# Key blocks of 56 + 8 keys, two heads on the partition halves, in an attention and mixture-of-experts kernel

## The chip, the cores and the metric

The kernel runs on one core of one Trainium2 chip. The metric is the device time of one execution in microseconds (us), lower is better. The core has a matrix engine (TensorE; PE in the profile, with its weight loads listed as PEld), a vector engine (VectorE, DVE), an activation engine (ScalarE, ACT), a general engine (GpSimd, POOL) and a queue (SP) from which this kernel starts nearly all of its DMA transfers. The engines run side by side; each takes its own instructions in program order.

## What is computed

Windowed attention with a few global keys, then a soft mixture of experts over the result:

```python
B, H, S, D = 4, 8, 768, 64          # batch, heads, positions, head size
scores = q @ k.T / sqrt(D)          # per batch and head, 768 x 768
rel  = pos[:, None] - pos[None, :]
keep = (pos[None, :] < 8) | ((rel >= 0) & (rel < 96))      # n_global = 8, n_local = 96
dist = where(is_global & ~is_local, 96, abs(rel))
a = softmax(where(keep, scores - slope[h] * dist, -1e9))
x = (a @ v) -> (B * S, 512)
logits = x @ phi                    # 8 experts x 4 slots = 32 columns
d = softmax(logits, over tokens);  c = softmax(logits, over slots)
slot_out[e] = relu((d.T @ x)[e] @ w1[e]) @ w2[e]           # 512 -> 1024 -> 512
out = c @ slot_out
```

A query sees its 96 most recent keys and the first 8, so of a 768 x 768 score matrix only a band and eight columns are needed.

## The kernel before

**Tiling of the attention.** The work is cut into 16 units `u`, one for each batch and pair of heads. For a unit, the keys are cut into NJ = 7 blocks of KB = 120 (the last has 48). A block of 120 keys is seen by the QW = 120 + 96 = 216 queries from its first key on. The 8 global keys ride along with every block, so a block has KR = 128 rows: 128 partitions of the score tile, with 216 queries along the free axis. A head has 5 x 216 + 168 + 48 = 1296 columns of this kind, a pair 2592.

**The steps of a unit**, each a function that `ORDER` calls by name:

- `load_qk`, `load_v`: SP starts the loads of queries and keys (two buffers, `raw0`, `raw1`) and of values (one buffer, `vraw`, line 420).
- `scores` (lines 530 to 539), in 3 pieces a unit: float32 matmuls on PE, contraction over the 64 rows of one head (the two heads lie on partitions 0 to 63 and 64 to 127), 128 keys out, written to PSUM with the head as bank. Each such matmul has two records in the trace.
- `biased` (line 548), 3 pieces: DVE adds the bias and mask table to the scores, writes SBUF (`tb0` to `tb2`) and keeps a running maximum; `max_t`, `max_r`, `max_b`, `max_c` turn that into one subtrahend for the unit.
- `exponential` (568, ACT), one a head. `w_hi` (578, ACT) rounds the weights to float16; `w_lo` (586, POOL, a few on DVE), 3 pieces a head, takes the float16 rest, so that three float16 products stand for a float32 one.
- `v_hi` (519 on POOL or 522 on ACT) and `v_lo` (527, DVE) split the values in the same way. Both read `vraw`, and the next `load_v` writes it.
- `values` (lines 591 to 603), one a head: for each of 7 tiles of 120 queries, the block of the same keys and the one before, times 3 products: 13 x 3 = 39 float16 matmuls with 128 rows of contraction and 65 or 64 columns.
- `ev_sum`, `ev_rec`, `ev_mul` (609, 613, 619, DVE): row sums, reciprocal, normalised output, for each head; `tr`, `tr_copy` (631, 636): transposes; `logits` (661) and, once a batch, the softmax over tokens and `dispatch` (736).

**Queues and order.** The order of all of this is written out by hand in the list `ORDER`; each engine and SP follow it. The list also places the loads of the expert weights: `piece` k (1 MB each) into one of NW = 12 tiles that are free from the start, and `free` i, which loads weight columns into a buffer of the attention as soon as its last user is done. `load_v` carries one small leftover piece.

**Buffers.** PSUM has 8 banks of 512 float32 columns. The score tiles take 4 (two tiles of two banks), the outputs of `values` one for each head, the rest two. There is one buffer `hi0` and one `lo0` for the split weights (NHB = 1), three for the biased scores (NTB = 3).

**After the attention**: `last_dispatch`, then `hidden` (line 119) with w1, `project` (149) with w2, `combine` (209 to 215), and the output.

```python
for i in range(2):                       # before, in scores: the heads of one block
    r = slice(D * i, D * i + D)
    nc.tensor.matmul(out=sc[:, i, at:at + n], lhsT=r_[r, KCOL[j]:KCOL[j] + KR],
                     rhs=r_[r, KW + KB * j:KW + KB * j + n], start=True, stop=True)
```

Of the kernel before, what the change touches and what calls it, by code (L numbers as in the profile page):

```python
# [23 lines left out]
NG = 8  # L24
KB = 120
P = 128
NJ = 7
KR = NG + KB
WIN = 96
QW = KB + WIN  # L30
QN = (QW,) * 5 + (S - 5 * KB, S - 6 * KB)
TN = tuple(min(KB, S - KB * j) for j in range(NJ))
BANK_J = ((0, 1), (2, 3), (4, 5, 6))
COL = tuple(sum(QN[:j]) for j in range(NJ))
BW = 2 * QW
TW = 3 * BW
TBW = 2 * TW
PB = KB + P
PCOL = tuple(PB * j for j in range(6)) + (PB * 5 + QN[5],)
PW = PCOL[6] + P  # L40
KW = NJ * KR
KCOL = tuple(KR * ((j + 5) % NJ) for j in range(NJ))
Q1 = KB + QW
# [4 lines left out]
XH = NJ * HF  # L48
VHW = NJ * 2 * (D + 1) // 2
VC = NJ * 2 * D  # L50
TABW = 4 * QW
NW = 12
NTB = 3
NHB = 1
# [6 lines left out]
P_EXP = 15  # L61
RS_MIN = 2.0 ** (P_EXP + 6 - 10)
RS_EPS = 1.0e-9 * RS_MIN
X_MIN = 2.0 ** -9


def homes(QKW, TBW, HPW, VC, VW, TABW, XH):
    return [
        ("wa", 12, dict(tab1=TABW, tab2=TABW, raw0=QKW, raw1=QKW, tab0=TABW, tab3=TABW, vraw=VC, tb1=TBW, tb2=TBW, tb0=TBW, v0=VW, v1=VW, hi0=HPW, lo0=HPW, xt1=S, xt2=S, xt0=S, xn2=XH)),
    ]  # L70


leaves = ('tab1', 'tab2', 'raw0', 'raw1', 'tab0', 'tab3', 'vraw', 'tb1', 'tb2', 'tb0', 'v0', 'v1', 'hi0', 'lo0', 'xt1', 'xt2', 'xt0', 'xn2')


T_SC = 0.125
TAB_UNIT = 0.5 / T_SC


class Moe:  # L80


    def __init__(self, tc, ident, sgn):
        self.nc, self.ident, self.sgn = tc.nc, ident, sgn

# [111 lines left out]
    def combine(self, ps, ct, n, sot, obs, out, t0, sizes):  # L197
# [4 lines left out]
        for size in sizes:  # L202
            obs.append(obs.pop(0))
            ob = obs[-1][:, 0:w * size]
            for m in range(0, size, 2):
# [5 lines left out]
                if (t0 + m) // 2 % 2 == 0:  # L211
                    nc.scalar.copy(out=dst, in_=cp)  # L212
                else:
                    nc.vector.tensor_copy(out=dst, in_=cp)  # L214
            nc.sync.dma_start(
                out=out[P * t0:P * (t0 + size), at:at + w].rearrange("(t p) f -> p t f", p=P), in_=ob.rearrange("p (t f) -> p t f", f=w))
            t0 += size


class BiasTable:  # L220

    def __init__(self, nc, tabs, space):

        self.nc, self.tabs = nc, tabs
        at = [0]

        def temp(rows, cols, dtype=F32):
            v = space[0:rows, at[0]:at[0] + cols]  # L230
            at[0] += cols
            return v if dtype == F32 else v.bitcast(dtype)

        def iota(rows, base, pattern, mult):
            i = temp(rows, pattern[1], I32)
            nc.gpsimd.iota(i, pattern=[pattern], base=base, channel_multiplier=mult)
            f = temp(rows, pattern[1])
            nc.vector.tensor_copy(out=f, in_=i)
            return f

        self.rel = iota(P, NG, [1, QW], -1)
        self.grel = iota(NG, 0, [1, QW], -1)
        self.gidx = iota(NG, 0, [0, 1], 1)
        self.other = temp(NG, QW)
        nc.gpsimd.memset(self.other, NEG)
        nc.gpsimd.memset(self.other[:, 0:KB], 0.0)
        self.base = temp(P, QW)
        self.t = temp(P, QW)
        self.g = temp(NG, QW)
        self.l = temp(NG, QW)  # L250
        self.s = temp(NG, 2)
        self.later = temp(P, QW // 2, BF16)
        nc.vector.tensor_scalar(out=self.t, in0=self.rel, scalar1=0.0, scalar2=NEG, op0=ALU.is_lt, op1=ALU.mult)
        nc.vector.scalar_tensor_tensor(out=self.base, in0=self.rel, scalar=-TAB_UNIT, in1=self.t, op0=ALU.mult, op1=ALU.add)

    def keys(self, ngl, nlo):
        nc = self.nc
        nc.vector.tensor_scalar(out=self.t, in0=self.rel, scalar1=nlo, scalar2=NEG, op0=ALU.is_ge, op1=ALU.mult)
        nc.vector.tensor_scalar(out=self.l, in0=self.grel, scalar1=nlo[0:NG], scalar2=NEG, op0=ALU.is_lt, op1=ALU.mult)
        nc.vector.tensor_scalar(out=self.s[:, 0:1], in0=self.gidx, scalar1=ngl[0:NG], scalar2=NEG, op0=ALU.is_ge, op1=ALU.mult)  # L260
        nc.vector.tensor_tensor(out=self.later, in0=self.base, in1=self.t, op=ALU.add)
        nc.vector.scalar_tensor_tensor(out=self.l, in0=self.grel, scalar=0.0, in1=self.l, op0=ALU.is_ge, op1=ALU.mult)
        nc.vector.scalar_tensor_tensor(out=self.s[:, 1:2], in0=nlo[0:NG], scalar=-TAB_UNIT, in1=self.s[:, 0:1], op0=ALU.mult, op1=ALU.add)

    def even(self):
        nc = self.nc
        t0, later = self.tabs[0][:, 0], self.later
        nc.vector.tensor_scalar(out=self.g, in0=self.other, scalar1=self.s[:, 1:2], scalar2=None, op0=ALU.add)
        nc.vector.tensor_copy(out=t0[:, 0:QW], in_=later)
        nc.vector.tensor_copy(out=later[0:NG], in_=self.g)  # L270
        nc.vector.tensor_tensor(out=t0[0:NG, 0:QW], in0=self.g, in1=self.l, op=ALU.add)
        nc.vector.tensor_copy(out=t0[:, QW:3 * QW].rearrange("p (j c) -> p j c", c=QW), in_=later.unsqueeze(1).to_broadcast([P, 2, QW]))
        for at, n in ((0, QN[5]), (QN[5], QN[6])):
            nc.vector.tensor_copy(out=t0[:, 3 * QW + at:3 * QW + at + n], in_=later[:, 0:n])

    def part(self, p, k):

        t = self.tabs[p]
        return bass.AP(tensor=t.tensor, offset=t.offset + QW * k, ap=[t.ap[0], [4 * QW, 2], [1, BW]])

    def odd(self):
        t = self.tabs[0]
        self.nc.vector.tensor_scalar(out=t[:, 1], in0=t[:, 0], scalar1=0.5, scalar2=None, op0=ALU.mult)

    def pair(self, p, act):
        if act:
            self.nc.scalar.activation(out=self.tabs[p], in_=self.tabs[0], func=AF.Copy, scale=0.25 ** p)
        else:
            self.nc.gpsimd.tensor_scalar(out=self.tabs[p], in0=self.tabs[0], scalar1=0.25 ** p, scalar2=0.0, op0=ALU.mult, op1=ALU.add)


@with_exitstack
def tile_attention_moe(ctx: ExitStack, tc: tile.TileContext, qk, v, phi, w1, w2, nn, out):
# [31 lines left out]
    QKW, HPW = S + KW, PW  # L325
# [27 lines left out]
    tabs = [own(f"tab{p}", TABW).bitcast(BF16).rearrange("p (i c) -> p i c", i=2) for p in range(NP)]  # L353
    by_head = "p (j i d) -> p j i d"
    vraw = own("vraw", VC).rearrange(by_head, j=NJ, i=2)
    v16 = [own(f"v{i}", VW) for i in range(2)]
    vhi = [w[:, 0:VHW].bitcast(F16).rearrange(by_head, j=NJ, i=2) for w in v16]
    vlo = [w[:, VHW:].bitcast(F16).rearrange(by_head, j=NJ, i=2) for w in v16]
    xn2 = own("xn2", XH)
    xnb = [a[0:KB].rearrange("p (t f) -> p t f", t=NJ) for a in (xn01[:, 0:XH], xn01[:, XH:], xn2)]  # L360
    xtb = [own(f"xt{i}", S) for i in range(3)]


    last = nu - 1
    spaces = []
# [40 lines left out]
    def free(i):  # L406
        for k, c0, c1 in spaces[i]:
            load_w([NW + held.index(k)], c0, c1)

    FIRST = slice(KCOL[0], KW + Q1)  # L410

    def load_qk0(u):
        nc.sync.dma_start(out=rq[0][:, FIRST], in_=qk[0, 0][:, FIRST])

# [28 lines left out]
    def blocks_of(w, i):  # L443
        return w[:, PW * i:PW * i + 6 * PB].rearrange("p (s c) -> p s c", c=PB)

# [696 lines left out]
```

## Time and profile before

| | us |
|---|---|
| median of 3 runs | 212.75 (211.31 to 213.36) |
| the profiled execution | 213.26 |
| its span, first to last instruction | 211.5 |
| start of `load_v` of units 1, 8, 15 | 13.95, 73.01, 126.51 |
| end of the last `ev_mul` (the attention is done) | 146.92 |
| start of `hidden` | 156.99 |

The page counts instructions in records; times are us unless marked ns. A row of the "costliest groups" gives line, engine, operation, output and input with partitions x elements, the count, then the busy time, the mean ns of one, and the idle time ahead of it with what ended it. Matmuls overlap, so the busy time of a group on PE is less than count times mean. The "chain of work that ended last" follows the waits back from the end. "Windows" give the busy time of each engine between two times, with the share of time in which the DMA engines were busy, and their GB/s.

### The profile page before, as it was taken

The numbers are of one execution on the slowest core, as the hardware profiler recorded it, in microseconds if no ns is written. First come the engines' busy times: TensorE is split into PE (matmuls) and PEld (weight loads), VectorE is DVE, ScalarE is ACT, GpSimd is POOL, SyncE is SP. The second block draws the span as 40 slices with busy tenths as digits, with TensorE's granted clock in tenths as the row PEclk, the third lists the DMA queues.
The fourth block names the chain that finished last, engine by engine and source line by source line (L and its number), as shares of the span: only waits on it lengthen the run. The fifth ranks groups of instructions, "written<-read, shape, count | busy, mean of one in ns | idle before, by whom it ended". The sixth has DMA issues, their size and how long they took to land.

```text
span 211.5 us, 6475 instructions
## 1 busy us (share of the span) xinstructions
PE 182.5 (86%) x2649; PEld 131.8 (62%) x2649; DVE 150.8 (71%) x375; ACT 127.6 (60%) x177; POOL 116.0 (55%) x141
## 2 busy tenths in 40 slices
PE   8679799986999989999999998887699999998400
PEld 2357688765787868878788876656253366576300
DVE  4889999658889878989988999296567835153600
ACT  2429899919589768979799989642403552042400
POOL 8436989785799796998889999840000000000000
PEclk9999999998899999999999999699999999999955
DMA  4769999997998976663487678998998999459892
GB/s 115 295 193 396 397 381 380 319 343 282 336 398 314 354 291 222 240 236 118 153 276 243 223 248 248 354 373 309 369 384 275 385 397 388 163 188 315 285 337 91
DMA packets 21063, 61.40 MB, mean 290 GB/s; under 512 B 2336, under 2 KB 9376, under 8 KB 19360
## 3 DMA queue, kind: packets, MB, share of 16 engines
q1 hardware_dynamic: 20880, 60.89, 79.8%
q8 instruction: 23, 0.38, 0.7%
q14 instruction: 16, 0.13, 0.2%
q10 hardware_dynamic: 144, 0.00, 0.0%
HBM read 54.59 MB, written 6.29 MB: 288 GB/s over the span
## 4 chain that ended last, share of the span: by engine, by line
PE 49%; DMA 18%; DVE 15%; POOL 9%; issue 3%; ACT 1%; DVEq 0%; POOLq 0%; SPq 0%
DMA wa<-in_v_dram 11%; PE x L602 11%; PE sc L538 9%; PE a L149 7%; PE hp L119 7%; POOL wa L586 6%; DVE wa L527 4%; PE m L631 3%; DMA wa<-in_qk_dram 3%; DVE wa L548 3%; PE m L736 2%; DMA out_dram<-wa 2%; DMA nraw<-in_n_dram 2%; POOL wa L519 2%; PE m L661 2%
## 5 line engine op out<-in xcount | busy, mean ns | idle before, releaser
L586 POOL TENSOR_TENSOR wa<-wa 128x432 f16<-128x432 f32 x91 | 98.4, 1111 | 12.3 <-ACT wa L578 8.1
L538 PE MATMUL sc<-wa 64*128 64x216 f32 (+2 forms) x448 | 49.3, 347 | 3.6 <-DVE mx L548 2.2
L602 PE MATMUL x<-wa 128*128 128x65 f16 (+1 forms) x1248 | 45.9, 196 | 3.5 <-POOL wa L586 2.0
L602 PEld LDWEIGHTS <-wa 128*128 128x128 f16 x1248 | 41.7, 99 | 9.6 <-issue 5.2
L578 ACT CAST wa<-wa 128x1296 f16<-128x1296 f32 x31 | 39.3, 1266 | 9.1 <-PE x L602 8.2
L538 PEld LDWEIGHTS sc<-wa 64*128 64x128 f32 x448 | 37.6, 190 | 10.6 <-DVE mx L548 4.1
L568 ACT ACTIVATE wa<-wa,nb 128x1296 f32<-128x1296 f32 x32 | 43.5, 1374 | 0.5
L548 DVE CUSTOM_DVE_ANT_1 wa<-sc,wa,mx 128x864 f32<-128x864 f32 x32 | 35.6, 1114 | 3.5 <-PE sc L538 1.0
L527 DVE SCALAR_TENSOR_TENSOR wa<-wa 128x896 f16<-128x896 f32 x16 | 24.3, 1519 | 5.5 <-ACT wa L522 3.1
L548 DVE CUSTOM_DVE_ANT_1 wa<-sc,wa 128x864 f32<-128x864 f32 x16 | 16.8, 1051 | 2.6 <-POOL wa L586 1.9
L636 ACT COPY wa<-m 128x480 f32<-128x480 f32 (+1 forms) x32 | 14.3, 473 | 6.7 <-PE m L631 6.7
L212 ACT COPY wa<-cp 128x512 f32<-128x512 f32 x12 | 6.3, 596 | 17.0 <-PE cp L209 15.3
L619 DVE CUSTOM_DVE_ANT_1 xn<-x,rc 120x448 f32<-120x448 f32 x24 | 14.9, 622 | 0.7
L522 ACT ACTIVATE wa<-wa 128x896 f16<-128x896 f32 x8 | 7.6, 951 | 11.4 <-DMA wa<-in_v_dram 10.5
L631 PE MATMUL m<-ident,xn 120*128 120x120 f32 x84 | 12.9, 276 | 1.1 <-DVE xmax L619 0.5
L519 POOL TENSOR_SCALAR wa<-wa 128x896 f16<-128x896 f32 x8 | 7.5, 941 | 10.7 <-DMA wa<-in_v_dram 8.4
L631 PEld LDWEIGHTS m<-ident,xn 120*128 120x128 f32 x84 | 8.6, 140 | 3.2 <-ACT wa L636 1.5
L119 PE MATMUL hp<-wp,sl 128*32 128x512 f32 x96 | 10.5, 593 | 0.0
L661 PE MATMUL m<-wa,phis 128*32 128x240 f32 (+1 forms) x128 | 9.5, 332 | 0.2 <-ACT wa L636 0.2
L214 DVE COPY wa<-cp 128x512 f32<-128x512 f32 x12 | 7.5, 682 | 2.1 <-PE cp L209 1.2
L609 DVE TENSOR_TENSOR rsall<-x,eps 120x7 f32<-120x7 f32 x32 | 5.0, 157 | 5.3 <-PE x L602 4.9
L561 PEld LDWEIGHTS m<-mm,bsel 2*128 2x128 f32 x32 | 4.7, 182 | 5.6 <-DVE mm L558 3.1
(163 smaller groups left out, 207.8 us busy)
## 6 DMA issues: line engine op xcount, KB each, us to landing
wa<-in_qk_dram SPq DMA_DIRECT2D x15, 832.0 KB, 6.6
wp<-in_w_dram SPq DMA_DIRECT2D x12, 1024.0 KB, 7.9
wa<-in_v_dram SPq DMA_DIRECT2D x16, 448.0 KB, 3.9
out_dram<-wa SPq DMA_DIRECT2D x12, 512.0 KB, 5.6
wp<-in_w_dram SPq DMA_DIRECT2D x8, 512.0 KB, 7.3
wp<-in_w_dram SPq DMA_DIRECT2D x16, 256.0 KB, 5.7
wa<-in_w_dram SPq DMA_DIRECT2D x3, 432.0 KB, 4.9
wa<-in_w_dram SPq DMA_DIRECT2D x1, 1024.0 KB, 6.8
```

Of the source, the lines that this page charges most:

```text
L119: nc.tensor.matmul(out=hp[n][32 * s:32 * s + 32, :], lhsT=slv(a, c, s), rhs=w1(e, c // 2)[:, (c % 2) * DF + 512 * n:(c % 2) * DF + 512 * n ...
L149: nc.tensor.matmul(out=o[32 * s:32 * s + 32, 0:w], lhsT=ht[:, c, 32 * s:32 * s + 32], rhs=w2(4 * a + s, half)[:, c0 + c * w:c0 + c * w + w ...
L527: nc.vector.scalar_tensor_tensor(out=vlo[k].rearrange(flat), in0=vraw.rearrange(flat), scalar=V_SC, in1=vhi[k].rearrange(flat)[:, :, 0:D], ...
L538: nc.tensor.matmul(out=sc[:, i, at:at + n], lhsT=r_[r, KCOL[j]:KCOL[j] + KR], rhs=r_[r, KW + KB * j:KW + KB * j + n], start=True, stop=True)
L548: nc.vector.tensor_tensor_reduce(out=tbs[u % NTB].rearrange("p (i c) -> p i c", i=2)[:, :, BW * k:BW * k + BW], in0=scs.pop((u, k))[:, :, ...
L568: nc.scalar.activation(out=head(u, i), in_=head(u, i), func=AF.Exp, bias=nbs[u], scale=T_SC)
L578: nc.scalar.copy(out=h, in_=t)
L586: (engine or nc.gpsimd).tensor_tensor(out=w, in0=t, in1=h, op=ALU.subtract)
L602: nc.tensor.matmul(out=x[:, (D + 1) * t:(D + 1) * t + d], lhsT=w[:, c:c + P], rhs=vv[:, j, i, 0:d], start=(z == 0), stop=(z == len(ops) - ...
L619: nc.vector.tensor_tensor_reduce(out=xnb[(u // 2) % 3][:, :, c:c + D], in0=out_of(u, i)[:, :, 0:D], in1=rcs.pop((u, i)).unsqueeze(2).to_br ...
L631: nc.tensor.transpose(out=m[:, at:at + KB], in_=xnb[(u // 2) % 3][:, t, P * (p % 2):P * (p % 2) + P], identity=ident[0:KB, 0:KB])
L636: nc.scalar.copy(out=xtb[u % 3][:, a:a + n], in_=ms.pop((u, k))[:, 0:n])
```

## The change

**Blocks.** KB is 56, so KR = 64, and there are NJ = 14 blocks. QW is 56 + 96 = 152. Twelve blocks see 152 queries, the last two (12 and 13) the QE = 96 last ones. The blocks form two groups, 0 to 5 with 12, and 6 to 11 with 13. A block's 64 rows of head 0 lie on one half of the partitions and those of head 1 on the other; `half(j, i)` swaps the halves for the second group. A group has GW = 6 x 152 + 96 = 1008 columns, a unit 2016.

**Scores** come in 2 pieces a unit of 2 x 504 columns, each with 16 matmuls of 64 rows of contraction and 64 keys out. **Bias** is 2 operations of 128 x 1008. `exponential` runs over a group (1008 columns). `w_hi` has 3 operations a unit (two of 912 columns, one of 192 for the ends of both groups), `w_lo` 5 (456, four times, and 192).

**Values** keep tiles of queries at TT = 112; each meets up to four blocks. There are 26 x 3 products a head, each over 64 rows. `values(u, k)` runs over group k for both heads, the heads in turn, each in its own PSUM bank; the two banks are one tile that `ev_sum` and `ev_mul` read, and `ev_rec` is once a unit.

**Buffers.** NHB = 2: two pairs `hi`, `lo`. The attention's buffers take 13 blocks of 1 MB in place of 12, and NW is 11. The table of the bias is built by other operations (`keys`, `even`, `odd`) for tiles of 704 words instead of 864.

**Order.** `ORDER` is new. Queries and keys of unit 0 are loaded by two DMAs (keys, queries) and not by a first part ahead; `load_qk(2)` stands ahead of `load_qk(1)`; pieces come about one a unit: between `load_v(1)` and `load_v(8)` there are pieces 0, 2 to 8 and `load_qk(3)` to `load_qk(11)`, where before there were pieces 1, 0, 2 to 9 and `load_qk(3)` to `load_qk(10)`. There are 20 `free` where there were 18.

```diff
-KB = 120
+KB = 56
+NJ = 14
+QE = S - 12 * KB
+HE = QE // 2
+GROUPS = ((0, 1, 2, 3, 4, 5, 12), (6, 7, 8, 9, 10, 11, 13))
-NW = 12
+NW = 11
-NHB = 1
+NHB = 2
+def half(j, i):
+    at = KR * (i ^ (j in GROUPS[1]))
+    return slice(at, at + KR)
...
     def scores(u, k):
-        scs[u, k] = sc = pss.tile([P, 2, 512], F32, name="sc", tag=f"s{(3 * u + k) % 2}")
+        scs[u, k] = sc = pss.tile([P, 2, 512], F32, name="sc", tag=f"s{k}")
         r_ = rq[u % 2]
+        for z in range(3 * k, 3 * k + 3):
+            for g in range(2):
+                product(sc, r_, g, GROUPS[g][z], 0, QW, (1 - k) * HE + QW * (z - 3 * k))
+        for g in range(2):
+            product(sc, r_, g, GROUPS[g][6], k * HE, HE, k * 3 * QW)
+
+    def product(sc, r_, g, j, c, n, at):
+        for i in range(2):
+            r = slice(D * i, D * i + D)
+            q = KW + QB[j] + c
+            nc.tensor.matmul(out=sc[half(j, i), g, at:at + n], lhsT=r_[r, KCOL[j]:KCOL[j] + KR], rhs=r_[r, q:q + n], start=True, stop=True)
...
+    def values(u, k):
+        ph, pl, vh, vl = whi[u % NHB], wlo[u % NHB], vhi[u % 2], vlo[u % 2]
+        if k == 0:
+            xps[u] = psx.tile([P, 2, 512], F32, name="x", tag="x")
         ops = []
+        for t in range(NTT):
+            for j in range(max(0, 2 * t - 2), 2 * t + 2):
+                if j not in GROUPS[k]:
+                    continue
...
         for z, (t, c, w, vv, j, d) in enumerate(ops):
+            for i in range(2):
+                r = half(j, i)
+                nc.tensor.matmul(out=xps[u][:, i, (D + 1) * t:(D + 1) * t + d], lhsT=w[r, c:c + P], rhs=vv[r, j, 0:d],
+                                 start=(k == 0 and z == 0), stop=(k == 1 and z == len(ops) - 1), skip_group_check=True)
...
-            out=xnb[(u // 2) % 3][:, :, c:c + D], in0=out_of(u, i)[:, :, 0:D], in1=rcs.pop((u, i)).unsqueeze(2).to_broadcast([KB, NJ, D]), scale=1.0,
+            out=xnb[(u // 2) % 3][:, :, c:c + D], in0=out_of(u)[:, i, :, 0:D], in1=rcs[u][:, i].unsqueeze(2).to_broadcast([TT, NTT, D]), scale=1.0,
...
     def load_qk(u):
-        for c in (slice(KW + Q1, KW + S), slice(0, KCOL[0])) if u == 0 else (slice(0, KW + S),):
+        for c in (slice(0, KW), slice(KW, KW + S)) if u == 0 else (slice(0, KW + S),):
             nc.sync.dma_start(out=rq[u % 2][:, c], in_=qk[u // NP, u % NP][:, c])
```

The bytes of the loads for a unit stay the same (832 KB of queries and keys, 448 KB of values), as does everything after the attention but for tiles of 112 tokens in place of 120.

More of the change, by code (lines that the diff above doesn't have):

```diff
@@ L57 @@
 NP = H // 2
-SW = 2 * KB
+SW = 2 * TT
 NEG = -1.0e30
@@ L241, in __init__ @@
[L241 to L253, printed above, removed]
@@ L265, in even @@
-    def even(self):
[L266 to L274, printed above, removed]
+        self.base, self.rel, self.t, self.later, self.f0, self.f1 = [temp(QW) for _ in range(6)]
@@ new lines, in __init__ @@
+        self.first = temp(QW)
+        ri = temp(QW, I32)
+        row, rowi = temp(1), temp(1, I32)
+        self.c = c = temp(8)
+        v = nc.vector
+        for z in range(2):
+            r = slice(KR * z, KR * z + KR)
+            nc.gpsimd.iota(ri[r], pattern=[[1, QW]], base=NG, channel_multiplier=-1)
+            nc.gpsimd.iota(rowi[r], pattern=[[0, 1]], base=0, channel_multiplier=1)
+            nc.gpsimd.memset(c[r, 4:5], 1.0 - 0.5 * z)
+            nc.gpsimd.memset(c[r, 5:6], 0.5 + 0.5 * z)
@@ new lines, in odd @@
+    def odd(self):
+        c, v, t = self.c, self.nc.vector, self.tabs[0]
+        two = bass.AP(tensor=t.tensor, offset=t.offset, ap=[t.ap[0], [TABN - HE, 2], [1, HE]])
+        v.tensor_scalar(out=two, in0=self.later[:, 0:QE].rearrange("p (z c) -> p z c", z=2), scalar1=c[:, 4:5], scalar2=None, op0=ALU.mult)
+        v.memset(t[:, TABN:TABN + HE], NEG)
+        v.memset(t[:, TABC - HE:TABC - QE + KB], NEG)
+        v.tensor_scalar(out=t[:, TABC - QE + KB:TABC], in0=self.later[:, 0:QE - KB], scalar1=c[:, 5:6], scalar2=None, op0=ALU.mult)
@@ L430, in load_phis @@
         nc.sync.dma_start(out=phis, in_=phi)
-    lnat = keep.tile([KB, 8 * B, NS], F32, name="lnat")
-    xmax = keep.tile([KB, B * H], F32, name="xmax")
-    rsall = keep.tile([KB, B * H, NJ], F32, name="rsall")
+    lnat = keep.tile([TT, 8 * B, NS], F32, name="lnat")
+    xmax = keep.tile([TT, B * H], F32, name="xmax")
+    rsall = keep.tile([TT, B * H, NTT], F32, name="rsall")
     state = keep.tile([P, 16], F32, name="state")
@@ L605, in out_of, with exponential @@
-    def out_of(u, i):
-        return xps[u, i][0:KB, 0:NJ * (D + 1)].rearrange("p (t d) -> p t d", d=D + 1)
-    def ev_sum(u, i):
-        nc.vector.tensor_tensor(out=rsall[:, 2 * u + i], in0=out_of(u, i)[:, :, D], in1=eps, op=ALU.add)
-    def ev_rec(u, i):
-        rcs[u, i] = wk.tile([KB, NJ], F32, name="rc", tag="rc", bufs=3)
-        nc.vector.reciprocal(out=rcs[u, i], in_=rsall[:, 2 * u + i])
+    def exponential(u, g):
+        w = tbs[u % NTB][:, GW * g:GW * g + GW]
+        nc.scalar.activation(out=w, in_=w, func=AF.Exp, bias=nbs[u], scale=T_SC)
@@ L615, in ev_mul, with out_of, ev_sum, ev_rec @@
+    def out_of(u):
+        return xps[u][0:TT, :, 0:NTT * (D + 1)].rearrange("p i (t d) -> p i t d", d=D + 1)
+    def ev_sum(u, k):
+        t = (slice(0, 3), slice(3, NTT))[k]
+        nc.vector.tensor_tensor(out=rsall[:, 2 * u:2 * u + 2, t], in0=out_of(u)[:, :, t, D], in1=eps[:, :, t], op=ALU.add)
+    def ev_rec(u):
+        rcs[u] = wk.tile([TT, 2, NTT], F32, name="rc", tag="rc", bufs=3)
+        nc.vector.reciprocal(out=rcs[u], in_=rsall[:, 2 * u:2 * u + 2])
     def ev_mul(u, i):
@@ L857, in tile_attention_moe @@
     fl = keep.tile([P, 12], F32, name="fl")
-    cst = keep.tile([KB, 8 * B, 4], F32, name="cst")
+    cst = keep.tile([TT, 8 * B, 4], F32, name="cst")
     def check_inputs():
@@ L1111, in _layout @@
         qk[..., a + NG:a + NG + n] = kt[..., KB * j:KB * j + n]
-        vl[:, :, :NG, j] = vt[:, :, :NG]
-        vl[:, :, NG:NG + n, j] = vt[:, :, KB * j:KB * j + n]
+        for i in range(2):
+            r = half(j, i).start
+            vl[:, :, r:r + NG, j] = vt[:, :, i, :NG]
+            vl[:, :, r + NG:r + NG + n, j] = vt[:, :, i, KB * j:KB * j + n]
     w2 = np.asarray(moe_w2, f32).reshape(E, 8, P, DM).transpose(0, 2, 1, 3)
```

280 lines of the change are left out of this document (137 added, 143 removed).

## Prediction

> **What bounds the kernel now.** I read the page's busy shares first, then windows cut at three starts of `load_v`, then the chain of waits in each of the two long windows.
>
> ```profile
> PE 182.5 (86%) x2649; PEld 131.8 (62%) x2649; DVE 150.8 (71%) x375; ACT 127.6 (60%) x177; POOL 116.0 (55%) x141
> ```
>
> ```profile
> 13.95 0.33 SPq L420 DMA_DIRECT2D wa<-in_v_dram  x1
> ...
> 73.01 0.33 SPq L420 DMA_DIRECT2D wa<-in_v_dram  x1
> ...
> 126.51 0.33 SPq L420 DMA_DIRECT2D wa<-in_v_dram  x1
> ```
>
> ```profile
> core 0: us, PE busy (x) PEld busy (x) DVE busy (x) ACT busy (x) POOL busy (x), PEclk, DMA share, GB/s
> 0.00:13.95 13.95, 10.10 (x56) 4.75 (x58) 10.08 (x31) 4.08 (x4) 8.40 (x36) 1.00 0.53 183
> 13.95:73.01 59.06, 54.22 (x846) 44.32 (x842) 50.26 (x118) 47.69 (x56) 46.78 (x46) 0.97 0.95 357
> 73.01:126.51 53.50, 52.62 (x903) 42.59 (x902) 46.92 (x114) 46.03 (x63) 48.20 (x49) 1.00 0.65 225
> 126.51:146.95 20.44, 17.03 (x296) 12.94 (x295) 14.74 (x40) 11.87 (x20) 12.62 (x13) 0.92 0.90 312
> 146.95:211.50 64.55, 48.50 (x556) 27.25 (x556) 28.80 (x75) 17.94 (x36) 0.00 (x0) 0.92 0.84 299
> ```
>
> Each of the two long windows holds seven units (loads of values 1 to 8 and 8 to 15): 8.44 us a unit early, 7.64 late. The last three columns are PE's granted clock, the DMA share and GB/s: early the DMA engines are 95% busy, late PE is (52.62 of 53.50). The chains say the same, first early, then late:
>
> ```profile
> by line: DMA wa<-in_v_dram 38.8%; DVE wa L527 13.2%; DMA wa<-in_qk_dram 11.3%; DVE wa L548 7.3%; PE sc L538 6.1%; POOL wa L519 4.8%; issue 3.4%; POOL wa L586 3.3%; ACT wa L522 3.3%; PE x L602 2.2%; POOL state L706 1.5%; DVE xn L619 1.3%; DV
> ...
> by line: PE x L602 30.7%; PE sc L538 29.6%; POOL wa L586 14.0%; PE m L631 10.2%; PE m L661 4.9%; PE m L736 3.4%; PE m L561 3.4%; PE m L555 3.1%; PE m L713 1.1%; issue 0.2%; POOLq L586 0.0%
> ```
>
> Early it is one loop: load of values, `v_hi`, `v_lo`, next load into the same buffer. Late it is PE's own program. A stretch of the late chain in order of time, and PE's time in `scores` and `values` in the late window:
>
> ```profile
> 110.26 1.28 PE x L602 x39
> 111.53 0.75 PE m L631 x7
> 112.29 1.00 PE sc L538 x12
> 113.29 1.29 PE x L602 x39
> ...
> 115.73 0.93 PE sc L538 x8
> ...
> 156.99 13.87 PE hp L119 x128
> ```
>
> ```profile
> 73.01:126.51 53.50, 18.33 (x170) 13.76 (x168) 1.00 0.65 225
> ...
> 73.01:126.51 53.50, 19.36 (x546) 17.60 (x546) 1.00 0.65 225
> ```
>
> `scores` (first row) takes 18.33 / 7 = 2.62 us a unit, `values` (second) 19.36 / 7 = 2.77.
>
> **The change: PE's scores.** One float32 record of 120 columns alone takes 0.75 / 7 = 107 ns (the transposes of L631), 0.89 ns a column. The 8 records of 216 columns of a piece would be 1.54 us one after the other and take 0.93: the two heads, on different rows of the array, run side by side. The 128 records of 512 columns at L119, on four column strips, would be 58 us and take 13.87, so four strips run side by side too. The new scores use both at once, rows by head and columns by half: four quarters of the array. That combination is in no row. A unit has 32 matmuls, 64 records, 4 x 1008 columns in two records each: 8064 x 0.89 = 7.18 us alone; in four quarters 1.79, in two 3.59. The old ones, 2 x 1296 x 2 x 0.89 = 4.61, halved 2.31, take 2.62, a factor 1.13. So the new ones take 2.03 (-0.59 a unit) or 4.07 (+1.45). I take -0.59, since rows and columns each overlap fully where a row shows them. `max_t` and the other small matmuls stay.
>
> **PE's values.** The products are halved in rows and doubled in number: 78 matmuls of 128 rows become 156 of 64 rows, in pairs on different rows. If the two of a pair run side by side as the heads of L538 do, 78 slots of 2.77 / 78 = 35.5 ns stay, and the cost is 0; nothing streams fewer columns, so there is no gain to be had. If they run one after the other, +2.77 a unit. I take 0 by L538; the ends are 0 and +2.77. Both outputs are now one tile, so `values(u+1)` waits for both `ev_mul`.
>
> ```profile
> L619 DVE CUSTOM_DVE_ANT_1 xn<-x,rc 120x448 f32<-120x448 f32 x24 | 14.9, 622 | 0.7
> L613 DVE RECIPROCAL rc<-rsall 120x7 f32<-120x7 f32 x32 | 6.3, 197 | 0.8
> L609 DVE TENSOR_TENSOR rsall<-x,eps 120x7 f32<-120x7 f32 x32 | 5.0, 157 | 5.3 <-PE x L602 4.9
> L548 DVE CUSTOM_DVE_ANT_1 wa<-sc,wa,mx 128x864 f32<-128x864 f32 x32 | 35.6, 1114 | 3.5 <-PE sc L538 1.0 <-DVE mx L548 0.5 <-POOL wa L586 0.4
> L578 ACT CAST wa<-wa 128x1296 f16<-128x1296 f32 x31 | 39.3, 1266 | 9.1 <-PE x L602 8.2
> L586 POOL TENSOR_TENSOR wa<-wa 128x432 f16<-128x432 f32 x91 | 98.4, 1111 | 12.3 <-ACT wa L578 8.1
> ```
>
> That wait is 0.16 + 0.20 + 2 x 0.62 = 1.6 us. On PE the scores (2.0) and transposes (0.75) of other units stand between and cover it; without them it costs 1.6 a unit at most, and I take 0.
>
> **The other engines.** The biased, exponentiated and split columns go from 2592 to 2016 a unit, x 0.78. In proportion DVE's bias goes from three operations near 1.11 to two of 1.30 (-0.7), ACT's casts from 2 x 1.27 to 1.97 in three operations (-0.5), POOL's `w_lo` from 6.3 (91 x 1.11 / 16) to 4.9 (-1.4). A fixed part in each operation would make the bias cheaper and the third cast dearer, by some 0.1 to 0.2. One reciprocal of 0.2 goes. Late these engines are busy 46.0 to 48.2 of 53.5, under PE, and stay under it; so nothing of this is counted in the late window. The second `hi` and `lo` takes away a wait of ACT for PE (8.2 us in all, in the row of L578), which is on no chain: 0, up to -1 where the pipeline drains at the end.
>
> **The late window**, then, is PE at 7.64 - 0.59 = 7.05 a unit: 49.4, -4.1.
>
> **The early window** is DMA. Between the starts of loads 1 and 8 SP's list has 10 pieces of 1024 KB, 8 loads of 832 KB and 7 of 448 before (20.0 MB, with a leftover of 73 KB), and 8, 9 and 7 after, with a leftover of 713 KB at `load_v(3)`: 19.5. At the same rate that is 59.06 x 0.97 = 57.4. At a DMA share of 1 it is 54.5. PE's need is 49.4. What bounds a unit is the loop on `vraw`; its DVE and POOL or ACT parts keep their size (896 columns), and a load waits for what is queued ahead, which is now at most a piece and a load of queries. I take 55 (-4), between the first two, for the DMA row is the nearest; the ends are 0 and -9.6.
>
> **Start.** DVE builds the bias table between these two rows:
>
> ```profile
> 5.61 0.33 DVE L258 TENSOR_SCALAR xn<-xn,nv 128x216 f32<-128x216 f32 x1
> ...
> 9.30 1.06 DVE L548 CUSTOM_DVE_ANT_1 wa<-sc,wa 128x864 f32<-128x864 f32 x1
> ...
> 13.38 1.00 PE L538 MATMUL sc<-wa 64*128 64x216 f32 x8
> ```
>
> ```profile
> wa<-in_qk_dram SPq DMA_DIRECT2D x15, 832.0 KB, 6.6
> ```
>
> The 14 operations there take 3.7 us, 0.26 each; the new `keys`, `even` and `odd` have 19 on mostly narrower columns, 4.9 at that mean: +1.2. The bias behind them loses 0.7, so `v_lo` of unit 0, and with it the load that opens the early window, comes +0.5 later. `load_qk(1)`, started at 2.6 before, now stands behind `load_qk(2)`, for which SP waits until the scores of unit 0 are done, near 8 us; with a landing of 6.6 it is there at 14.6. The first scores of unit 1 ran at 13.38; while they are late DVE still has `v_lo`. Ends 0 and +1.2; I take +0.5.
>
> **End and tail.** The window from 126.51 to 146.95 holds the scores of two units (-1.2) and the drain of the last one, w_hi and w_lo on 78% of the columns (-0.3): -1.5. The tail is PE at `hidden` and `project`, with DMA at 84%. One place for a piece fewer at the start and 13 blocks that come free late in place of 12 move 1 MB towards it: 1.05 MB at 299 GB/s is 3.5 us if PE waits for all of it; the DMAs have some 16% to spare: +0.5, ends 0 and +3.5.
>
> **Sum.** 211.5 - 4.0 - 4.1 + 0.5 - 1.5 + 0.5 = 202.9. The profiled execution took 213.26, 1.76 over its span and 0.51 over the median of 212.75: 202.9 + 1.76 - 0.51 = 204.2.
>
> **Rivals.** *Scores in two lanes* (slower). The two heads of a block now write different partitions of one PSUM bank, where before each had its own bank. If rows that share a bank take turns, scores cost +1.45 and a unit takes PE 9.09: 63.6 in each long window (+4.6, +10.1), +2.4 at the end, +1.0 at start and tail: 230.9. It decides once the overlap falls under three lanes (7.18 x 1.13 / 2.62 = 3.1). For it speaks that no row shows such a pair; against it that L119's strips share a bank and overlap. 13%. [...]
>
> *Values issued too slowly* (about as before, or slower). If a product has a cost of its own that a pair cannot share, the 35.5 ns of a pair grow; halfway to one after the other a product takes 26.6, +1.39 a unit, PE 8.44: 59.1 in both windows (0, +5.6), +1.3, +1.0: 220.6. From about 23 ns a product on the gain is gone. Against it: the records and weight loads of L538 go side by side. 18%, over 209 to 221. [...]
>
> *Values wholly one after the other* (slower): +2.77, PE 9.82: 68.7 in both windows, 242.6. 4%.
>
> *The loop on `vraw` gives way as well* (faster): PE bounds the early window too, 49.4, and the tail is covered: 211.5 - 9.6 - 4.1 + 0.5 - 1.5 + 1.25 = 198.0. For it: less is queued ahead of each load. Against: 95% DMA. 7%.
>
> **The numbers.** The forecast has 58%, with 199 to 209 by its own terms. From 195 to 220 lie it, nearly all of the second rival and the last one, some 80%. One per cent, about what a measurement here can tell from no change, is 2.1 us: of the second rival 3 points are faster, 6 the same and 9 slower; so faster 58 + 7 + 3, same 6, slower 13 + 4 + 9.
>
> **What would show it.** Scores near 2.0 us a unit on PE, two pieces of about 1.0 each; values near 2.8; seven units from load 8 to load 15 in about 49.5 and from 1 to 8 in about 55; PE still 95% busy late. Scores at 4 or values over 3.5 would make it wrong, and so would an early window of 59 at a lower DMA share, which would say that the loop's latency binds and not its bytes.

## The result: slower by 12%, and the profile after

| | before | after |
|---|---|---|
| median (lowest to highest) | 212.62 (211.31 to 213.36) | 240.58 (236.19 to 243.49) |
| the profiled execution, its span | 213.26, 211.5 | 242.31, 240.5 |
| `load_v` of units 1, 8, 15 | 13.95, 73.01, 126.51 | 14.74, 89.58, 153.47 |
| TensorE instructions a unit in the two long windows | 250 | 487 |

The medians are of four runs each; the ratio, 1.117 with an interval of 1.107 to 1.128, leaves out disturbed runs as all ratios here do, of the changed kernel the two over 242, one of which is the profiled execution. The forecast was 204.2, with a range of 195 to 220.

The windows of the changed kernel, cut as before at `load_v` of units 1, 8 and 15 (columns as before):

```profile
0.00:14.74 14.74, 11.02 (x89) 5.06 (x89) 11.25 (x40) 3.81 (x4) 9.12 (x43) 0.88 0.38 129
14.74:89.58 74.84, 56.03 (x1701) 47.88 (x1704) 42.17 (x100) 43.65 (x68) 39.34 (x43) 0.91 0.76 280
89.58:153.47 63.89, 54.96 (x1707) 44.65 (x1701) 40.62 (x96) 42.43 (x71) 39.04 (x41) 0.92 0.63 213
153.47:240.50 87.03, 64.64 (x997) 39.52 (x989) 38.79 (x105) 25.72 (x52) 5.41 (x7) 0.88 0.82 289
```

Of the 29.0 us that the span grew, 15.8 lie in the early window and 10.4 in the late one. In neither is an engine full any more: PE is busy for 55 of 64 us late, the DMA engines for 76% early. The instruction counts are the PE and PEld counts of the windows, (1701 + 1704 + 1707 + 1701) / 14 = 487 a unit; the same sum of the windows before gives 250.

The waits of the changed kernel, longest first (engine and line, what it waited for, us in all, times, longest):

```profile
POOL wa L611 <- ACT wa L602: 52.1, 25, 6.3
DVE rsall L644 <- PE x L635: 39.9, 28, 4.8
ACT wa L672 <- PE m L667: 33.5, 18, 6.5
PEld L635 <- issue: 26.4, 23, 4.0
ACT nb L585 <- PE m L581: 22.4, 11, 6.2
PE x L635 <- issue: 21.5, 12, 3.9
```

The other engines wait for PE, directly or through ACT, and PE waits for "issue", which the profile writes where an engine stood still with nothing to wait for. A stretch of the chain of waits shows such a place (start, us, what):

```profile
44.08 1.04 PE sc L562 x32
45.11 0.31 PE m L581 x2
45.42 1.04 PE sc L562 x32
46.46 0.41 PE x L635 x20
46.87 1.10 issue
47.97 1.06 PE x L635 x58
...
50.17 1.05 PE x L635 x61
51.23 3.92 issue
55.15 0.59 PE x L635 x17
...
71.63 1.30 PE x L635 x78
```

The reader is to see two things. The work itself has the forecast durations: a piece of scores takes 1.04 us, an uncut call of values, with its 78 products, 1.30. And another call is cut in the middle, after 61 of its 78 products, without any input missing: its other 17 products read the same tiles.

Numbering PE's matmuls, weight loads and semaphore steps in the order of the trace, 14 of the 15 gaps over 1 us between numbers 300 and 8000 lie at a number that is 192 modulo 256 (the other waits on a semaphore); the kernel before has no gap over 0.2 us at any of its 20 numbers of that kind. The page, before and after, has a DMA queue that carries instructions, in packets of 16 KB (packets, MB, share). Its 23 and 37 packets are near one for every 256 of PE's numbers, 5350 before and 9013 after:

```profile
q8 instruction: 23, 0.38, 0.7%
```

```profile
q8 instruction: 37, 0.61, 1.0%
```

Set against the packets of that queue, from the records of the changed kernel:

```
PE enters page  next fetch starts  lands   PE enters next page  standstill  MB of loads outstanding at entry
 31.68           35.74              36.67    38.02                3.36        2.05
 47.96           52.93              53.90    55.15                4.11        1.54
 64.35           67.58              68.53    69.89                1.54        1.31
 69.89           71.11              72.33    73.73                0.01        0.13
100.57          101.62             102.55   104.21                0.11        0.15
157.35          162.36             163.32   164.74                2.28        1.14
```

"Outstanding" are the bytes of the loads that SP has started by then, less those that the packets have moved. In all of this kernel's 31 fetches up to 190 us, the fetch of a page of 256 instructions started only after PE had entered the one ahead of it: 0.2 to 1.6 us after (median 1.1) with under 0.2 MB of loads outstanding, and 3.2 to 5.0 us after with 1.1 to 2.1 MB (delay = 1.18 us + 1.55 us a MB, correlation 0.86). It took 1.0 on the mean, and where PE stood still, it went on 1.2 to 2.0 us after the landing, 1.4 in the median. An estimate from these: a page mostly needs 3.4 to 7.4 us; the shortest here took 2.9. The new kernel uses 487 / 256 = 1.90 pages a unit, at the forecast 7.05 us a unit one every 3.7 us; the old one used one every 9.0 us early (241 a unit of 8.44) and 7.6 late (258 of 7.64). The 23 gaps at page ends that are over 0.2 us sum up to 36.0 us.

In these traces the long standstills go with a lower clock. The trace also records the clock that PE was granted, 1.00 or 0.50. In the changed kernel each of the four standstills of over 3 us, those that end at 38.02, 55.15, 127.97 and 157.35, has a stretch of half clock that begins between 1.1 us before its end and 0.3 after it, and lasts 3.4 or 6.8 us; of the eight between 1.5 and 3 us, three have one within 2 us of their end. Half clock was granted for 13.7 us of the early window (6.8 of them behind the wait for unit 1's queries, shown below) and 10.2 of the late one, and for none of the late window before (3.4 us of the early one). An estimate from this: up to half of that time, 7 and 5 us, went to slower work.

### The profile page after: what moved, and what is told of

Read it like the earlier page. It is cut to its first block, busy times and chain, and to the rows that moved or that the text cites. A ratio compares the mean times of both kernels' runs of the same rounds, so it can differ in the third digit from the quotient of the medians.

```text
span 240.5 us, 10069 instructions
## 1 busy us (share of the span) xinstructions
PE 186.7 (78%) x4476; PEld 137.1 (57%) x4476; DVE 132.8 (55%) x338; ACT 115.6 (48%) x193; POOL 92.9 (39%) x132
## 4 chain that ended last, share of the span: by engine, by line
PE 71%; issue 14%; DMA 6%; DVE 3%; ACT 0%; SPq 0%; DVEq 0%
PE x L635 20%; PE sc L562 16%; PE a L157 6%; PE m L667 6%; PE hp L127 6%; DMA wa<-in_qk_dram 5%; PE m L772 3%; PE m L697 3%; PE m L581 2%; PE m L575 2%; DMA out_dram<-wa 1%; PE ctp L191 1%; PE cp L217 1%; DVE wa L568 1%; PE ld L772 1%
## 5 line engine op out<-in xcount | busy, mean ns | idle before, releaser
L611 POOL TENSOR_TENSOR wa<-wa 128x456 f16<-128x456 f32 (+1 forms) x75 | 75.4, 1026 | 55.5 <-ACT wa L602 52.1
L635 PE MATMUL x<-wa 64*128 64x65 f16 (+1 forms) x2496 | 49.7, 196 | 22.2 <-issue 21.5
L635 PEld LDWEIGHTS <-wa 64*128 64x128 f16 x2496 | 44.3, 98 | 28.8 <-issue 26.4
L562 PE MATMUL sc<-wa 64*64 64x152 f32 (+1 forms) x1024 | 41.6, 303 | 8.9 <-DMA wa<-in_qk_dram 5.4
L562 PEld LDWEIGHTS sc<-wa 64*64 64x64 f32 x1024 | 36.8, 149 | 15.5 <-issue 12.9
L602 ACT CAST wa<-wa 128x912 f16<-128x912 f32 (+1 forms) x47 | 34.1, 749 | 10.2 <-PE x L635 9.0
L589 ACT ACTIVATE wa<-wa,nb 128x1008 f32<-128x1008 f32 x32 | 36.1, 1135 | 0.3
L672 ACT COPY wa<-m 128x448 f32<-128x448 f32 (+1 forms) x32 | 14.9, 480 | 33.7 <-PE m L667 33.5
L568 DVE CUSTOM_DVE_ANT_1 wa<-sc,wa 128x1008 f32<-128x1008 f32 x16 | 19.3, 1205 | 13.7 <-PE sc L562 13.0
L568 DVE CUSTOM_DVE_ANT_1 wa<-sc,wa,mx 128x1008 f32<-128x1008 f32 x16 | 20.2, 1265 | 4.8 <-POOL wa L611 2.5
L667 PE MATMUL m<-ident,xn 112*128 112x112 f32 x84 | 14.3, 297 | 2.8 <-issue 2.4
```

The lines of the kernel that those rows point to most:

```text
L562: nc.tensor.matmul(out=sc[half(j, i), g, at:at + n], lhsT=r_[r, KCOL[j]:KCOL[j] + KR], rhs=r_[r, q:q + n], start=True, stop=True)
L568: nc.vector.tensor_tensor_reduce(out=tbs[u % NTB].rearrange("p (g c) -> p g c", g=2)[:, :, BW * k:BW * k + BW], in0=scs.pop((u, k))[:, :, ...
L589: nc.scalar.activation(out=w, in_=w, func=AF.Exp, bias=nbs[u], scale=T_SC)
L602: nc.scalar.copy(out=w, in_=t)
L611: (engine or nc.gpsimd).tensor_tensor(out=w, in0=t, in1=h, op=ALU.subtract)
L635: nc.tensor.matmul(out=xps[u][:, i, (D + 1) * t:(D + 1) * t + d], lhsT=w[r, c:c + P], rhs=vv[r, j, 0:d], start=(k == 0 and z == 0), stop=( ...
```

## The experiments

The theory: PE starves for instruction pages; their number a unit nearly doubled, and a fetch waits behind queued loads. The rivals: the new order and its waits; the granted clock (0.899 after 0.961); the loop on `vraw`; something in products of half the rows. "Standstills" below are gaps at page ends over 0.2 us, summed from each kernel's trace.

| kernel | instructions a unit | standstills | median (range) |
|---|---|---|---|
| before | 250 | 0 | 212.62 |
| after | 487 | 36.0 | 240.58 |
| queries of unit 1 first | 486 | 28.9 | 240.94 (237.23 to 245.99) |
| weights behind the attention | 489 | 19.1 | 240.03 (236.26 to 241.56) |
| weights in rows of 2 KB | 486 | 25.9 | 239.16 (232.25 to 247.11) |
| values of 128 rows, both calls | 333 | 5.8 | 211.88 (206.74 to 213.48) |
| values of 128 rows, one call of two | 410 | 16.1 | 221.52 (218.57 to 224.61) |
| values of 128 rows, queries of unit 1 first | 335 | 3.8 | 208.70 (207.08 to 212.62) |
| the same, weights behind the attention | 335 | 0.7 | 226.63 (one run) |
| before, values cut in two | 400 | 16.5 | 225.36 (221.19 to 230.04) |
| before, values cut in four | 681 | 65.2 | 300.07 (296.76 to 304.01) |

The kernel before was timed again beside the runs: 213.57 beside rows three to six, 212.48 beside rows seven, eight, ten and eleven, 215.05 (one run) beside row nine. The first expectation on values gives 555 and 400 instructions a unit; counted from the windows they are 487 and 333.

### Half the instructions, same work on the array

This kernel, like all rows with values of 128 rows, mixes the heads and leaves out half of the sums, so only its time says something. One more line, not shown, keeps the flag of the fallback off.

```diff
-            for i in range(2):
-                r = half(j, i)
-                nc.tensor.matmul(out=xps[u][:, i, (D + 1) * t:(D + 1) * t + d], lhsT=w[r, c:c + P], rhs=vv[r, j, 0:d],
-                                 start=(k == 0 and z == 0), stop=(k == 1 and z == len(ops) - 1), skip_group_check=True)
+            nc.tensor.matmul(out=xps[u][:, z % 2, (D + 1) * t:(D + 1) * t + d], lhsT=w[:, c:c + P], rhs=vv[:, j, 0:d],
+                             start=(k == 0 and z < 2), stop=(k == 1 and z >= len(ops) - 2), skip_group_check=True)
...
```

> The two products of a pair (64 rows each, one for each head) become one product of all 128 rows, written to the two heads' banks in turn, and the fallback's flag stays off; so the values mix the heads and half the products' sums are left out, at the same TensorE time a product (35.5 ns before) and half the instructions: about 400 instead of 555 TensorE instructions a unit. Theory (instruction supply): a page of 256 instructions then lasts 4.6 us instead of 3.2, most fetches are hidden, the standstills fall from 34 us to under 10, the seven units late take 50 to 53 instead of 63.9, the whole 207 to 215. Rival A (order and waits for inputs), rival B (lower granted clock) and rival C (the loop on vraw): the order, loads and streamed columns are the same, so 235 or more. Rival D (64-row values cost more than 128-row ones): the values alone shrink, by what the calls' durations shrink (under 3 us in all).

It took 211.88 us, 0.980 of the kernel before (0.969 to 0.991), so whether it is 2% faster stays open; the changed kernel's loss is gone. Its two long windows:

```profile
14.47:76.17 61.70, 52.61 (x1210) 45.51 (x1213) 43.59 (x100) 44.40 (x69) 41.48 (x43) 0.94 0.90 342
76.17:131.73 55.56, 49.67 (x1125) 41.88 (x1118) 40.52 (x96) 41.78 (x70) 40.91 (x40) 0.97 0.68 232
```

The order, the loads, the waits and the streamed columns stayed; an uncut call of values takes 1.29 to 1.30 us, as in the changed kernel. The span fell by 28.8 us and the standstills by 30.2. That rules out the order, the loop on `vraw` and the clock as the main cause. The late window, 55.6, is 2.6 over the range that was expected; the last experiment takes that up.

### A middle dose

The same edit for the first of a unit's two calls of values only.

> Only the first call of values of each unit becomes products of all 128 rows (heads mixed, half of its sums left out, the fallback's flag off); the second keeps its pairs of 64. 78 instructions a unit fewer: 408 instead of 486. Theory (instruction supply): halfway or less, standstills of 12 to 22 us between the 36 and the 6 already seen, the time 219 to 229. Rival (something else in the pairs of 64 rows, by its own time): the uncut second call keeps the whole of its loss, and the calls with pairs are longer than 1.3 us where no 256th instruction falls into them.

221.52 us, 1.033 of before (1.021 to 1.045), standstills 16.1: between the two. The two kinds of call, 128 rows and pairs of 64, in this kernel (count, busy time, mean ns of a record, idle time ahead):

```profile
L634 PE MATMUL x<-wa 128*128 128x65 f16 (+1 forms) x624 | 24.2, 200 | 4.8 <-issue 3.2 <-DVE xmax L658 1.6
L639 PE MATMUL x<-wa 64*128 64x65 f16 (+1 forms) x1248 | 24.2, 196 | 2.3 <-issue 2.3
```

1248 products in pairs are busy exactly as long as 624 of all rows, so a pair costs what one product costs, and the pairs are not the ones that stand still more. The rival of the pairs' own time falls.

### The converse: more instructions in the kernel before

```diff
-            nc.tensor.matmul(out=x[:, (D + 1) * t:(D + 1) * t + d], lhsT=w[:, c:c + P], rhs=vv[:, j, i, 0:d],
-                             start=(z == 0), stop=(z == len(ops) - 1), skip_group_check=True)
+            for h in range(0, P, 64):
+                nc.tensor.matmul(out=x[h:h + 64, (D + 1) * t:(D + 1) * t + d], lhsT=w[:, c + h:c + h + 64], rhs=vv[:, j, i, 0:d],
+                                 start=(z == 0), stop=(z == len(ops) - 1), skip_group_check=True)
```

The second kernel has 32 in place of 64.

> The kernel before, with each product of values cut into two of 64 stationary columns, side by side on the array's column halves; the same computation, layout, loads and order, 156 more TensorE instructions a unit (406 in place of 250). Theory (instruction supply): a page of 256 then lasts 5.3 us early and 4.8 late at the old pace, and needs 3.4 to 7.4 by what is queued, so standstills at every 256th instruction appear where there were none: 8 to 20 us in sum, the time 218 to 232, the calls of values that no standstill cuts still near 1.3 us. Rival (it is the new layout, the row halves or the new order that hold TensorE, not the count of instructions): 210 to 216, no standstills at every 256th.

> The same with four products of 32 stationary columns: 468 more instructions a unit, 718 in all, 2.8 pages. Theory: each page needs 3.4 to 5 us on the mean, so a unit takes 9.5 to 14 us whatever TensorE could do, the time is 260 to 310, and the standstills are 50 us or more. Rival (layout, halves, order): 210 to 220. Rival (each product has an issue cost of its own, without pages): the calls of values grow evenly, with no standstill at every 256th.

225.36 us (1.051, 1.037 to 1.066) and 300.07 us (1.406, 1.389 to 1.423). The old layout, order and loads are untouched, and the standstills appear, at the same place: all 16 gaps over 1 us of the second kernel between numbers 300 and 8000 are at 192 modulo 256. A stretch of its chain, and its waits for "issue":

```profile
100.00 0.49 PE x L603 x59
100.49 0.56 PE m L632 x4
101.05 1.00 PE sc L538 x12
102.06 0.32 PE x L603 x25
102.37 0.62 issue
103.00 1.22 PE x L603 x119
104.22 3.60 issue
107.82 0.24 PE x L603 x3
```

```profile
PEld L603 <- issue: 58.7, 43, 4.6
...
PE x L603 <- issue: 50.0, 26, 4.5
```

The last call is cut in three, after 25 and after 153 of its 156 products (of the 128 in the middle the chain names 119); the first two parts run at 9.5 to 13 ns a product, and PE then stops for 3.6 us three products before the end. It is not a cost of each product: the cost sits at the page. With the layout, the order and the row halves of the kernel before, the rivals that blame these fall.

### The loads behind which a fetch waits

In `ORDER` every `piece` and `free` moves behind the last step of the attention, and the leftovers are loaded there too:

```diff
     def load_v(u):
         nc.sync.dma_start(out=vraw, in_=v[u // NP, u % NP])
-        if u > 2 and extras:
-            k, c0, c1 = extras.pop(0)
-            load_w([k], c0, c1)
```

> All loads of expert weights that stood among the attention's steps (piece, free, the leftovers at load_v) move behind the last of them; same computation. During the attention only qk and v are loaded, 1280 KB a unit. Theory (instruction supply, and a fetch waits behind the loads that are queued when it starts): fetches start about 1.1 to 2.5 us after they are due instead of up to 5.0, a page needs 3.4 to 5, so the seven units early take 52 to 58 (74.8 in the changed kernel) and late 51 to 56 (63.9); the tail then waits for some 20 MB more of weights, so the whole is 225 to 245. Rival C (the loop on vraw: DMA bytes): early shrinks, late stays at 62 to 65. Rivals A and B (order, clock): both windows stay within 3 us.

```profile
15.40:75.98 60.58, 54.27 (x1703) 46.83 (x1707) 43.01 (x100) 43.58 (x69) 40.74 (x43) 0.92 0.51 172
75.98:133.43 57.45, 52.58 (x1719) 43.52 (x1713) 40.08 (x96) 42.84 (x70) 40.07 (x41) 0.97 0.39 134
```

Both windows shrank, by 14.3 and 6.4 us, with 3410 and 3432 instructions (3405 and 3408 in the changed kernel); they are 2.6 and 1.5 us over the ranges that were expected. The mean delay of a fetch in them fell from 2.5 to 1.7 us, with 0.4 MB outstanding on the mean in place of 0.9. In them the standstills went from 27.8 to 12.3 us. The late one shrank too, which the loop on `vraw` does not explain. What is left has the form foretold for a short queue: the shortest way from one page to the next stays over 3.1 us. The tail gives the gain back (106.4 us from `load_v` of unit 15 on, 87.0 in the changed kernel), since it now waits for the weights, whose loads are 35% of the whole chain, and the whole stays at 240.03.

```diff
-            nc.sync.dma_start(out=places[k][:, c0:c1], in_=(w1, w2)[m][e][:, WP * half + c0:WP * half + c1])
+            for a in range(c0, c1, 512):
+                b = min(c1, a + 512)
+                nc.sync.dma_start(out=places[k][:, a:b], in_=(w1, w2)[m][e][:, WP * half + a:WP * half + b])
```

> Each load of expert weights is cut into loads of 512 columns (2 KB a row in place of up to 8 KB); same bytes, same places, same computation. Theory, form 1 (a fetch waits for the bytes queued ahead of it): nothing changes, 236 to 243, delays of 4 to 5 us stay. Form 2 (a fetch waits for a number of packets ahead of it, in turns between the queues): the delays fall to about a quarter over 1.1 us, at most 2, standstills fall to 15 us or less and the time to 220 or less.

239.16 us, from 232.25 to 247.11: the single run under 236 aside, no change can be told. The delays stay, up to 4.6 us, against MB outstanding at 0.60 us + 2.00 us a MB (correlation 0.84), so the number of packets is not what counted here. Over the fetches before 190 us in the ten kernels other than the one before:

```
MB of loads outstanding at the page's entry   fetches   mean delay, us
under 0.2                                        56        1.07
0.2 to 0.6                                       56        1.43
0.6 to 1.0                                       62        2.40
1.0 to 1.4                                       44        3.08
1.4 to 3.5                                       60        3.59
over 3.5 (4.1 to 7.8)                             6        3.29
```

The delay grows up to some 1.4 MB and then no more: the six fetches with 4.1 to 7.8 MB outstanding waited 2.0 to 3.9 us. So not all that was queued stood ahead of these fetches. Single fetches scatter widely, 0.1 to 5.0 us in the first row and 0.8 to 5.5 in the fifth. In the kernel before no such link shows: five fetches with over 2 MB outstanding started 0.5 to 3.2 us after the entry. PE never waited for a page there; what sets the delays in it was not looked into.

### The order of the first loads

```diff
 ('warm', 0, 8),
+('load_qk', 1),
 ('load_qk', 2), ('table_even', 0), ('v_hi_act', 0), ('table_odd', 0),
-('load_qk', 1),
 ('biased', 0, 0),
```

> load_qk(1) goes back ahead of load_qk(2) in the order; nothing else changes. Theory (TensorE starves for instructions: it stands still at each 256th of its instructions until the next 16 KB have been fetched): the gap before the first scores of unit 1 (18.54 in the changed kernel) closes, they start near 15, and the span falls by about 3 us, to about 237 of 240.5; the standstills at every 256th instruction stay, about 34 us in sum. Rival A (it is the new order of loads and steps that holds TensorE, and the standstills are waits for its inputs): setting right the most visible fault of the order takes 10 us or more off.

In the changed kernel the chain of waits at the start shows what the order cost:

```profile
11.88 0.33 SPq L438
12.21 0.04 issue
12.25 6.15 DMA wa<-in_qk_dram
18.40 0.14 issue
18.54 1.49 PE sc L562 x17
```

With the edit unit 1's scores start at 15.07, 3.5 us earlier, and `load_v` of unit 8 at 86.14, 3.4 earlier. But the time did not fall as expected: 240.94. In the profiled execution the late window took 65.65 instead of 63.89, and PE was busy for 193.2 us instead of 186.7 at a granted clock of 0.868 instead of 0.899. Whether a kernel that starves does not keep an earlier start, or the scatter (237 to 246) hides 3 us, these runs do not tell. No 10 us came off: rival A falls.

> Both repairs in one: the values as products of all 128 rows (heads mixed, half of the sums left out, the fallback's flag off) and load_qk(1) ahead of load_qk(2). Theory: the late start of unit 1 (3.1 us) no longer hides behind standstills, so 2 to 4 us come off the 211.9 of the values alone: 207 to 210. Rival (the values' loads, late behind weights, hold what is left): no gain, 210.5 to 213.

With few instructions the same edit took 208.70 against 211.88. That is no gain shown: the two ranges overlap, and against the kernel before, timed beside each, the ratios are 0.983 (0.973 to 0.992) with the edit and 0.980 (0.969 to 0.991) without it.

### What is left without standstills and without a queue

> Values as products of all 128 rows (heads mixed, half of the sums left out, the fallback's flag off), load_qk(1) first, and all weights' loads behind the attention: neither many instructions nor a long queue of loads. Theory (after the standstills, what keeps the two windows over PE's own 49.4 are loads of queries and values that wait behind weights): both windows of seven units come down to 49 to 52, from 61.6 and 53.6 of the kernel with both repairs; the tail waits for the weights, so the whole is 222 to 236. Rival (the new order itself makes TensorE wait for the other engines): the windows stay over 54 early and 53 late.

```profile
15.43:68.57 53.14, 50.92 (x1213) 44.23 (x1216) 43.80 (x100) 44.54 (x70) 43.55 (x43) 0.97 0.59 195
68.57:117.71 49.14, 47.19 (x1132) 40.21 (x1124) 41.35 (x96) 41.38 (x69) 39.54 (x41) 1.00 0.45 153
```

The late window is 49.14, PE's own need as forecast (49.4); the early one is 53.14, a little over the 49 to 52 expected. So the new order does not hold PE. With the weights among the attention's steps the same kernel took 61.59 and 53.58, 8.5 and 4.4 us more (one profiled execution each). Of these, 2.8 and 2.2 are busy time of PE, at clocks of 0.92 and 0.97 in place of 0.97 and 1.00; the rest are standstills (some 2 and 0.6) and loads that wait behind weights, of queries early (17.3% of that window's chain) and of values late (28.9%). Of the kernels that compute the reference, none was faster than the one before; a way to have the new layout's values with fewer products was not tried.

## Why the prediction was wrong

**The step that failed** is "PE's values": "78 slots of 2.77 / 78 = 35.5 ns stay, and the cost is 0". The slots did stay (1.30 us an uncut call of 39 pairs; 19.69 / 566 = 34.8 ns a slot in the late window of the last experiment), but the cost of doubling the products was set at nothing without naming what hides it. What hid it was the time that a page of 256 instructions lasted before, 7.6 to 9.0 us. With 487 instructions a unit it lasts 3.7 at PE's own pace and needs 3.4 to 7.4. The instruction queue stood in the page before the change (23 packets), and I did not count instructions. In its place the runs showed 36.0 us of standstills, of which 16.7 lie in the early window, 11.1 in the late one and 8.2 behind them.

The prediction took PE at its late pace throughout; the half clock behind long standstills, by the estimate above up to 7 and 5 us of the two windows, was no term of it either.

**Right in the mechanism, by luck in the size:** the scores. Four quarters run side by side: 2 x 1.04 = 2.08 us an uncut unit where 2.03 was forecast. But the 2.62 that the forecast started from was misread. A unit of scores had 28 records, so the 170 of the late window are 6.1 units and not seven, 3.02 us each; the factor is then 1.31, not 1.13, and the same sum gives 2.34. The scores of the late window, before and in the last experiment:

```profile
73.01:126.51 53.50, 18.33 (x170) 13.76 (x168) 1.00 0.65 225
```

```profile
68.57:117.71 49.14, 13.06 (x384) 11.70 (x384) 1.00 0.45 153
```

With 64 records a unit the second row is 6 units of 2.18. So a unit saved 0.84 and not 0.59, but on six units and not seven: 5.0 us in place of 4.1.

The rival "scores in two lanes" falls: the two heads of a block write one bank, and an uncut unit took 2.08 us where the estimate for turns was 4.07. The two misreadings nearly cancel, so the forecast of 49.4 for the late window, were it PE's alone, came close in the last experiment (49.14).

**The other engines** came out as forecast: bias 1.21 and 1.27 us (1.30), `w_lo` 75 x 1.03 / 16 = 4.8 a unit (4.9), casts 47 x 0.75 / 16 = 2.2 (1.97 and some 0.1 to 0.2). They are off the chain: DVE has 3% of it, ACT and POOL next to nothing.

**The early window** (55 forecast, 74.84 measured) is off for two reasons: the standstills, and waiting loads, 61.59 in the kernel with both repairs, where the share of the DMA engines was 0.86 and not near 1. My bound from bytes was 6.6 us too kind, of which some 2.8 are standstills.

**The start.** The loads' window opened at 14.74, +0.8 where +0.5 was forecast with ends 0 and +1.2. But the late queries of unit 1 held its scores until 18.54, 3.5 us longer than with the other order; what that cost in the whole, the runs do not tell. What was mis-sized is the start of that load: it was issued at 12.3 and landed at 18.4, not at the 14.6 worked out, since SP waited for the scores of unit 0 until 11.87 and not until "near 8".

**End and tail** (-1.5 and +0.5 forecast) came to +2.0 (87.03 from `load_v` of unit 15 on, 84.99 before), with 8.2 us of standstills in them; with both repairs they take 80.16, so the terms were too small, not too large.

**The rivals.** "Values issued too slowly" was the nearest, with a cost that a pair cannot share; its price of 26.6 ns a product is refuted (1.30 us for 78 products, 16.7 ns each), and its 220.6, which like 230.9 lacks the 0.51 that the forecast takes off, is 20 short. No rival had the fetch of instructions.

## What to carry to other kernels

When a change cuts matmuls into more and smaller ones, count TensorE's instructions (matmuls and weight loads) and divide the stretch's time by the number of pages of 256: here a page every 5.4 us at PE's pace lost 4 to 6 us in all (333 instructions a unit), one every 5.1 cost 5% (the kernel before with 400), and one every 3.7 cost 12%. Array time that stayed the same was not enough here. Look at the loads queued beside it: with 1.4 MB or more outstanding a page's fetch started some 2.5 us later than with next to none, so large prefetches and small instructions got in each other's way.

## What the hardware showed that was not expected

A fetch of 16 KB of instructions started later the more loads were outstanding, 1.1 us after the page's entry with under 0.2 MB and 3.6 with 1.4 to 3.5, and no later with more (3.3 with over 3.5); rows of 2 KB in place of up to 8 left that as it was.

PE's granted clock fell where it stood still often: 1.00 in the late window before, 0.92 after, and 0.84 with products cut in four. A stretch of that kernel shows its scores after two standstills:

```profile
64.83 2.09 issue
66.92 1.22 PE x L603 x125
68.14 2.78 issue
71.68 3.32 PE sc L538 x20
```

20 records take 3.32 us, 166 ns each, where the 12 at 101.05 took 83 ns each; the trace grants half clock from 68.5 to 75.3. So behind these standstills a record took twice as long. That it is the standstills that lower the clock was not tried by itself: the evidence is where the half clock lies.
